# Attention followed by a SwiGLU block on one core: the attention output of batches 2 to 7 transposed by DMA through DRAM scratch, not by TensorE

## The chip, the cores and the metric

The kernel runs on one core of a Trainium2 chip. Its time is the device time of one execution in microseconds; the kernel before takes 408.24 us (median of 3 runs, 408.18 to 408.55). The core has a matrix engine (TensorE, PE in the profile), a vector engine (VectorE, DVE), an engine for activation functions (ScalarE, ACT), a general one (GpSimd, POOL), and a sync engine (SyncE, SP) that here only issues DMA transfers, in order. SBUF and PSUM are the on-chip memories; matmuls write to PSUM, which the kernel uses as 8 banks of 128 x 512 float32.

## What is computed

Causal attention with an extra bias from a running sum of `s`, in 8 batches of 8 heads, 576 positions of 64 elements; its output, with the heads of a position side by side, is the 4608 x 512 input of a gated feed-forward block (FFN). From the reference, shortened:

```python
# q, k, v: (8, 8, 576, 64), s: (8, 8, 576)
scores = scale * np.matmul(q, k.transpose(0, 1, 3, 2))
cum = np.cumsum(np.maximum(s, 0.0), axis=-1)
bias = -(cum[:, :, :, None] - cum[:, :, None, :])
scores = np.where(causal, -1000000000.0, scores + np.minimum(bias, 0.0))
attn = softmax(scores)                       # written out in the reference
attn_out = np.matmul(attn, v)
x = attn_out.transpose(0, 2, 1, 3).reshape(B * S, H * D)      # 4608 x 512
# w_gate, w_val: 512 x 1536; w_out: 1536 x 512
g = x @ w_gate
silu = g * (1.0 / (1.0 + np.exp(-g)))
out = (silu * (x @ w_val)) @ w_out           # 4608 x 512, float32
```

## The kernel before

The FFN works on 9 tiles of 512 tokens. Its first matmuls need `x` with the 512 features on the partitions, as `xt` (128 partitions x 4 pairs of heads x 512 tokens), while attention leaves the output of a pair of heads as `ot`, with the tokens on the partitions. So each pair's output has to be transposed. A batch has 576 tokens, so the pair's columns go to two tiles: batch `b` gives the last `512 - 64 b` tokens of tile `b` and the first `64 + 64 b` of tile `b + 1`.

Attention for one head is cut into pieces (4 of scores, 3 of the product with `v`), and a generator yields after each with its position in heads (`kk + 0.1` and so on). The FFN loop emits its own matmuls in 36 steps a tile and after each pumps the generator up to a target, so that the pieces of batch `tt + 1` stand between the matmuls of FFN tile `tt`. `LAG` is how many heads attention is to be ahead of the bare minimum when a tile starts. All engines run their instructions in the order of emission.

```python
def av_out(bh):                       # normalise one head: PSUM -> ot
    pr, e = divmod(bh, 2)
    if e == 0:
        ots[pr] = otp.tile([128, NCH, 2 * D], BF16, tag="ot", name="ot")
    ...
    nc.vector.reciprocal(rc, av3[:, :, D])                       # L401
    nc.vector.tensor_mul(ot[:, :, e * D : (e + 1) * D], ...)     # L402

def x_pe(pr):                         # transpose one pair: ot -> xt
    b, r = divmod(pr, H // 2)
    ot = ots.pop(pr)
    for tt in ((0, 1) if b == 0 else (b + 1,)):
        if r == 0:
            xts[tt] = xtp.tile([128, 4, TT], BF16, tag="xt", name="xt")
    bs = take()
    ps = view16(bs, S)
    for c in range(NCH):              # 5 chunks: 4 of 128 tokens, 1 of 64
        n = 128 if c < 4 else TAIL
        nc.tensor.transpose(                                     # L420
            ps[:, c * 128 : c * 128 + n], ot[0:n, c, :], ident[0:n, 0:n]
        )
    n0 = TT - 64 * b
    nc.vector.tensor_copy(xts[b + 1][:, r, 0 : S - n0], ps[:, n0:S])   # L424
    nc.vector.tensor_copy(xts[b][:, r, TT - n0 : TT], ps[:, 0:n0])     # L425
    give(bs)

def attn_items():
    for kk in range(H, BH + 2):
        h, step = divmod(kk, HB)
        if kk < BH:
            ...                       # scores of head kk; side(h, step): loads, casts,
                                      # scratch writes and DMA transposes of q and k
        x = kk - 2
        if x >= H and x % 2 == 1:
            x_pe(x // 2)
            yield kk + 0.5
        p = kk - 1
        if H <= p < BH:
            av_piece(p, (0, 1, 2))    # L385
            yield kk + 0.6
            av_piece(p, (3,))
            yield kk + 0.7
            av_piece(p, (4,))
            av_out(p)
            yield kk + 0.8

def ffn_items(tt):
    xt = xts[tt]
    for ft in range(NFT):             # 12 times
        for c in range(4):            # c: pair of heads
            nc.tensor.matmul(pg, WG[j][:, c, f0 : f0 + 128], xt[:, c, :], ...)  # L518
        ...                           # tanh on ScalarE, products on VectorE
        yield 1
        for c in range(4):
            nc.tensor.matmul(pv, WV[j][:, c, f0 : f0 + 128], xt[:, c, :], ...)  # L533
        ...
        yield 1
    for ts_ in range(4):              # 4 output blocks of 128 tokens
        for ft in range(NFT):
            nc.tensor.matmul(py, hts[ft][:, ts_ * 128 : (ts_ + 1) * 128], WO..., ...)  # L546
            ...
        nc.scalar.mul(ysb, py, 0.5)                              # L554
        nc.sync.dma_start(out[...], ysb)                         # L556
        yield 1

LAG = 1.65
for tt in range(NTT):
    lo = H * (tt + 1) + (LAG if tt else 0)
    hi = min(H * (tt + 2) + LAG, BH + 2)
    ...                               # pump from lo to hi over the 36 steps of tile tt
```

The scores are L347, their exponentials L360. From the sixth half batch on, q and k (as bfloat16) already go through DRAM scratch: GpSimd casts them, a DMA writes `ks` and `qs` (L244), and DMA transposes bring them back as `pk` and `pq` (L254). All of these are issued on the sync engine's queue.

Of the kernel before, what the change touches and what calls it, by code (L numbers as in the profile page):

```python
# [13 lines left out]
BF16 = mybir.dt.bfloat16  # L14
# [5 lines left out]
def kernel(  # L20
# [11 lines left out]
    nc = tc.nc  # L32
    PSUM = bass.MemoryType.PSUM

    B, H, S, D = q.shape
    NT, DM = out.shape
    DF = moe_w_gate.shape[1]
    BH = B * H
    NCH = 5
    TAIL = S - 512  # L40
# [5 lines left out]
    TT = 512  # L46
# [17 lines left out]
    def pt_col(tj, bi):  # L64
# [10 lines left out]
    xtp = ctx.enter_context(tc.tile_pool(name="xtp", bufs=3))  # L75
    hpool = ctx.enter_context(tc.tile_pool(name="hpool", bufs=3))
    yp = ctx.enter_context(tc.tile_pool(name="yp", bufs=3))
    dram = ctx.enter_context(
        tc.tile_pool(name="dram", bufs=1, space=bass.MemoryType.DRAM)
    )  # L80

    NPE = 5
    KS = {i: dram.tile([NR * S, 128], BF16, name=f"ks{i}") for i in range(NPE, NHB)}
    QS = {i: dram.tile([NR * S, 128], BF16, name=f"qs{i}") for i in range(NPE, NHB)}

    WG = [const.tile([128, 4, WCH], BF16, name=f"wg{j}") for j in range(NWCH)]
# [14 lines left out]
    with tc.manual_schedule():  # L101
# [14 lines left out]
        def take(kind="s"):  # L116
            b = min((x for x in bank if x[0] == kind), key=lambda x: released[x])
            assert released[b] < OPEN
            released[b] = OPEN
            return b  # L120

        def give(b):
            clock[0] += 1
            released[b] = clock[0]
# [15 lines left out]
        def view16(b, w):  # L140
            return bank[b][:, 0 : w // 2].bitcast(BF16)
# [12 lines left out]
        def load_qk(hb):  # L154
            load_one(hb, "k")
            load_one(hb, "q")
# [66 lines left out]
        def cast_one(hb, name, eng):  # L223
            cts[name, hb] = cp.tile([128, J, NR, D], BF16, tag="c" + name, bufs=2, name="c" + name)
            dst = cts[name, hb].rearrange("x j r d -> x r j d")
            src_t = loaded[name, hb]
            if eng is nc.scalar:
                nc.scalar.copy(dst, src_t)
            else:
                eng.tensor_copy(dst, src_t)  # L230
# [11 lines left out]
        def scratch(hb):  # L242
            for name, SC in (("k", KS), ("q", QS)):
                nc.sync.dma_start(  # L244
                    SC[hb].rearrange("(x j) c -> x (j c)", j=J),
                    cts[name, hb].rearrange("x j r d -> x (j r d)"),
                )
# [3 lines left out]
        def transposes(hb):  # L251
            for name, SC in (("k", KS), ("q", QS)):
                prs[name, hb] = cp.tile([128, NR * S], BF16, tag="p" + name, bufs=1, name="p" + name)
                nc.sync.dma_start_transpose(prs[name, hb], SC[hb])  # L254

        def split(hb, name, eng):
            kq = SRC[name][1]
            for r in range(NR):
                eng.tensor_copy(
                    KQ[hb % 2][r][64 * r : 64 * r + 64, kq, 0 : NR * S],  # L260
                    prs[name, hb][64 * r : 64 * r + 64, :],
                )
# [56 lines left out]
        ots = {}  # L319
        xts = {}  # L320
# [72 lines left out]
        def av_out(bh):  # L393
# [3 lines that stand above are left out]
            ot = ots[pr]  # L397
            av, bs = avs.pop(bh)
            av3 = av.rearrange("p (c e) -> p c e", e=D + 1)
            rc = small.tile([128, NCH], FP32, tag="rc", name="rc")  # L400
            nc.vector.reciprocal(rc, av3[:, :, D])  # L401
            nc.vector.tensor_mul(  # L402
                ot[:, :, e * D : (e + 1) * D],
                av3[:, :, 0:D],
                rc[:, :, None].to_broadcast([128, NCH, D]),
            )
            give(bs)
            pts.pop(bh)

        def x_pe(pr):  # L410
            b, r = divmod(pr, H // 2)
            ot = ots.pop(pr)
            for tt in ((0, 1) if b == 0 else (b + 1,)):
                if r == 0:
                    xts[tt] = xtp.tile([128, 4, TT], BF16, tag="xt", name="xt")
            bs = take()
            ps = view16(bs, S)
            for c in range(NCH):
# [9 lines that stand above are left out]
        def side(h, step):  # L428
# [8 lines left out]
            if h >= 3 and h + 3 < NHB and step == 0:  # L437
                load_qk(h + 3)
            if h + 1 < NHB and h + 1 >= NPE:
                if step == 0:  # L440
                    split(h + 1, "k", nc.vector)
                    aug(h + 1, SP4)
                if step == 1:
                    split(h + 1, "q", nc.vector)
            if h + 2 < NHB and h + 2 >= NPE:
                if step == 1:
# [32 lines left out]
# [4 lines that stand above are left out]
                    if step == 3 and h + 2 < NPE:  # L483
                        cast_one(h + 2, "k", nc.gpsimd)
                        cast_one(h + 2, "q", nc.gpsimd)
                    if step == 0 and 3 < h + 1 < NPE:
                        aug(h + 1, SP4)
                    for ci in range(4):
                        score_piece(kk, ci)
                        if ci == 1:  # L490
                            side(h, step)
                        yield kk + 0.1 + ci / 8
                        if h + 1 < NPE and (step, ci) in PREP_AT:
                            prep_one(h + 1, PREP_AT[step, ci])
                            yield kk + 0.1 + ci / 8
                x = kk - 2
                if x >= H and x % 2 == 1:
                    x_pe(x // 2)
                    yield kk + 0.5
                p = kk - 1  # L500
                if H <= p < BH:
                    av_piece(p, (0, 1, 2))
                    yield kk + 0.6
                    av_piece(p, (3,))
                    yield kk + 0.7
                    av_piece(p, (4,))
                    av_out(p)
                    yield kk + 0.8

        def ffn_items(tt):  # L510
# [111 lines left out]
        first_batch()  # L622
        second_psum()
        at = attn_items()
        state = {"pos": float(H)}

# [4 lines left out]
                except StopIteration:  # L631
                    state["pos"] = 1e9

        LAG = 1.65
        hook = {
            1: [lambda: cast_one(2, "k", nc.gpsimd), lambda: cast_one(2, "q", nc.vector)],
            2: [lambda: prep_one(2, 0)],
# [4 lines left out]
            21: [lambda: load_qk(5)],  # L642
        }
        for tt in range(NTT):
            lo = H * (tt + 1) + (LAG if tt else 0)
            hi = min(H * (tt + 2) + LAG, BH + 2)
            span = 36
            n0 = 7 if tt == 0 else 0
            n = 0
            for _ in ffn_items(tt):  # L650
                n += 1
                for f in hook.pop(n, ()):
                    f()
                pump(lo + (hi - lo) * min(1.0, max(0, n - n0) / (span - n0)))
# [31 lines left out]
```

The softmax here doesn't subtract the row's maximum and nothing guards it: scores larger than these inputs give would overflow.

## Time and profile before

| | |
|---|---|
| time, median of 3 | 408.24 us (408.18 to 408.55) |
| span of the profiled execution | 406.5 us |
| granted TensorE clock, mean | 0.987 |
| DMA moved | 56.71 MB, 140 GB/s in the mean |
| DMA packets | 85288, of which 65489 under 512 B |
| from one FFN tile's first matmul to the next, steady part | 42.1 us |

A group of the profile's fifth part is read like this: line, engine, operation, output from input, count, then busy time and mean length of one, then the idle time of the engine just before them and who ended it. For the operations that are changed:

```profile
L402 DVE TENSOR_TENSOR ot<-bank,rc 128x320 bf16<-128x320 f32 x56 | 27.5, 492 | 1.9
L424 DVE COPY xt<-bank 128x128 bf16<-128x128 bf16 (+6 forms) x28 | 9.0, 321 | 31.7 <-PE bank L420 31.0
```

The 31.7 us before L424 is VectorE's idle time, not TensorE's. Tiles are named after the buffers in the code; `bank` and `one` are PSUM banks.

### The profile page before, as it was taken

The page shows a single profiled execution, that of the slowest core. Times are in us where ns is not written, and L with a number is a line of the kernel's source. Part 1 is how long each engine was busy: PE and PEld are TensorE (multiplying, and loading weights), DVE is VectorE, ACT ScalarE, POOL GpSimd, SP SyncE. Part 2 cuts the span into 40 slices and gives each one's busy share as a digit, 9 for nine tenths or more (in the row PEclk, how much of TensorE's full clock was granted, in tenths as well). Part 3 has the DMA queues.
Part 4 walks back from the last instruction along what each step waited for, and adds up shares of the span by engine and source line. Part 5 has one row for each costly group of instructions (what it writes and reads, how often), then busy time and mean ns, then how long its engine had stood idle before and what let it go on. Part 6 is the DMA issues. An engine that isn't in the chain of part 4 may idle for free.

```text
span 406.5 us, 8052 instructions
## 1 busy us (share of the span) xinstructions
PE 384.8 (95%) x3100; PEld 213.0 (52%) x3100; DVE 249.1 (61%) x487; ACT 212.0 (52%) x407; POOL 125.0 (31%) x225
## 2 busy tenths in 40 slices
PE   2778799999999999999999999999999999999996
PEld 2664355655555555555555555555555554444442
DVE  7755658547863696368835784489447733852760
ACT  6742566855555655555545654655555542322321
POOL 6852444732442235222613162316211110000000
PEclk9988899999999999999999999999999999999999
DMA  7999899398635784579356944681510002002002
GB/s 242 188 250 212 267 192 269 133 272 190 178 93 194 174 206 118 173 194 211 102 157 192 247 72 127 214 167 51 120 57 0 2 27 78 0 16 89 2 1 103
DMA packets 85288, 56.71 MB, mean 140 GB/s; under 512 B 65489, under 2 KB 69553, under 8 KB 85249
## 3 DMA queue, kind: packets, MB, share of 16 engines
q1 hardware_dynamic: 81440, 51.44, 47.0%
q0 software_dynamic: 3808, 4.76, 6.9%
q8 instruction: 24, 0.39, 0.4%
q14 instruction: 16, 0.12, 0.1%
HBM read 37.90 MB, written 15.93 MB: 132 GB/s over the span
## 4 chain that ended last, share of the span: by engine, by line
PE 89%; DVE 4%; ACT 2%; DMA 2%; POOL 1%; issue 1%; ACTq 0%; SPq 0%
PE bank L546 23%; PE bank L518 22%; PE bank L533 22%; PE bank L347 9%; PE bank L385 7%; PE bank L420 3%; PE wide L347 1%; DMA kq<-HL 1%; PE one L385 1%; DMA s_sb<-in_s_dram 1%; ACT th L523 1%; POOL vt L171 1%; DVE pp L525 1%; DVE kq L301 1%; ACT pt L360 1%
## 5 line engine op out<-in xcount | busy, mean ns | idle before, releaser
L360 ACT ACTIVATE pt<-bank 128x512 bf16<-128x512 f32 x224 | 104.2, 505 | 42.4 <-PE bank L347 35.1
L525 DVE SCALAR_TENSOR_TENSOR pp<-th,bank 128x512 bf16<-128x512 bf16 x108 | 74.2, 687 | 65.2 <-ACT th L523 64.6
L518 PE MATMUL bank<-xt,wg 128*128 128x512 bf16 x432 | 112.1, 382 | 0.7 <-DVE xt L425 0.7
L533 PE MATMUL bank<-xt,wv 128*128 128x512 bf16 x432 | 112.5, 383 | 0.0
L523 ACT ACTIVATE th<-bank 128x512 bf16<-128x512 f32 x108 | 64.5, 597 | 81.6 <-PE bank L518 79.8
L546 PE MATMUL bank<-wo,ht 128*128 128x512 bf16 x432 | 105.7, 379 | 0.0
L363 POOL TENSOR_SCALAR_AFFINE_SELECT pt<-pt 128x512 bf16<-128x512 bf16 x64 | 40.8, 638 | 127.1 <-ACT pt L360 124.7
L538 DVE TENSOR_TENSOR ht<-pp,bank 128x512 bf16<-128x512 bf16 x108 | 73.8, 684 | 7.4
L347 PE MATMUL bank<-kq 128*128 128x128 bf16 (+4 forms) x504 | 66.7, 241 | 3.3 <-DVE kq L301 2.5
L347 PEld LDWEIGHTS <-kq 128*128 128x128 bf16 x576 | 46.1, 100 | 40.2 <-issue 4.2
L518 PEld LDWEIGHTS <-wg 128*128 128x128 bf16 x432 | 38.6, 98 | 36.9 <-issue 1.9
L533 PEld LDWEIGHTS <-wv 128*128 128x128 bf16 x432 | 38.9, 99 | 35.2 <-issue 1.7
L546 PEld LDWEIGHTS <-ht 128*128 128x128 bf16 x432 | 38.1, 98 | 34.9
L385 PEld LDWEIGHTS <-pt 128*128 128x128 bf16 x960 | 41.1, 98 | 19.0 <-issue 1.9
L385 PE MATMUL bank<-vt,pt 128*128 128x65 bf16 x840 | 44.0, 194 | 0.0
L554 ACT ACTIVATE ysb<-bank 128x512 f32<-128x512 f32 x36 | 21.5, 597 | 42.9 <-PE bank L546 41.4
L368 POOL TENSOR_SCALAR_AFFINE_SELECT pt<-pt 128x64 bf16<-128x64 bf16 x64 | 15.3, 239 | 63.4 <-ACT pt L360 60.7
L402 DVE TENSOR_TENSOR ot<-bank,rc 128x320 bf16<-128x320 f32 x56 | 27.5, 492 | 1.9
L424 DVE COPY xt<-bank 128x128 bf16<-128x128 bf16 (+6 forms) x28 | 9.0, 321 | 31.7 <-PE bank L420 31.0
L401 DVE RECIPROCAL rc<-bank 128x5 f32<-128x5 f32 x56 | 10.6, 190 | 25.2 <-PE bank L385 25.2
L171 POOL CAST vt<-rawv 128x512 bf16<-128x512 f32 (+1 forms) x40 | 25.8, 673 | 0.0
L230 POOL CAST ck<-rawk 128x1152 bf16<-128x1152 f32 x15 | 17.4, 1159 | 11.5 <-DMA rawk<-in_k_dram 11.5
(59 smaller groups left out, 191.6 us busy)
## 6 DMA issues: line engine op xcount, KB each, us to landing
out_dram<-ysb SPq DMA_DIRECT2D x36, 256.0 KB
rawk<-in_k_dram SPq DMA_DIRECT2D x15, 576.0 KB
rawq<-in_q_dram SPq DMA_DIRECT2D x15, 576.0 KB
rawv<-in_v_dram SPq DMA_DIRECT2D x32, 256.0 KB
ks<-ck SPq DMA_DIRECT2D x11, 288.0 KB
qs<-cq SPq DMA_DIRECT2D x11, 288.0 KB
wg<-in_moe_w_gate_dram POOLq DMA_DIRECT2D x2, 768.0 KB, 12.0
wv<-in_moe_w_val_dram POOLq DMA_DIRECT2D x2, 768.0 KB, 13.6
```

The lines of the kernel that those rows point to most:

```text
L171: eng.tensor_copy(VT[b % 2][0:n, c, :, 0:D], loaded["v", b][0:n, c, :, :])
L347: nc.tensor.matmul(sc[:, o : o + w], T[:, 1, e * S + 128 * tj : e * S + 128 * (tj + 1)], T[:, 0, e * S + lo : e * S + hi], start=True, sto ...
L360: nc.scalar.activation(pt[:, c0 : c0 + W], sc[:, 0:W], AF.Exp, scale=0.125)
L363: nc.gpsimd.affine_select(pt[:, 1088:1600], pt[:, 1088:1600], pattern=[[0, 4], [1, 128]], compare_op=ALU.is_ge, fill=zreg, base=0, channel ...
L385: nc.tensor.matmul(av[:, bi * (D + 1) : (bi + 1) * (D + 1)], pt[:, c0 : c0 + 128], VT[b % 2][:, tj, h, :], start=(tj == 0), stop=(tj == bi),)
L402: nc.vector.tensor_mul(ot[:, :, e * D : (e + 1) * D], av3[:, :, 0:D], rc[:, :, None].to_broadcast([128, NCH, D]),)
L518: nc.tensor.matmul(pg, WG[j][:, c, f0 : f0 + 128], xt[:, c, :], start=(c == 0), stop=(c == 3),)
L523: nc.scalar.activation(th, pg, AF.Tanh, scale=0.5)
L525: nc.vector.scalar_tensor_tensor(pp, in0=th, scalar=1.0, in1=pg, op0=ALU.add, op1=ALU.mult)
L533: nc.tensor.matmul(pv, WV[j][:, c, f0 : f0 + 128], xt[:, c, :], start=(c == 0), stop=(c == 3),)
L538: nc.vector.tensor_mul(ht, pp, pv)
L546: nc.tensor.matmul(py, hts[ft][:, ts_ * 128 : (ts_ + 1) * 128], WO[ft // WKO][:, ft % WKO, :], start=(ft == 0), stop=(ft == NFT - 1),)
```

## The change

From batch 2 on (`XB = 2`), a pair's output isn't transposed by TensorE. `x_out` writes `ot` to a DRAM scratch `XS` of 576 x 128 with two DMAs, once both heads are normalised. `x_in` later reads it back with two DMA transposes, straight into the two `xt` tiles. That takes the transposes from TensorE, the copies from VectorE and the bank from PSUM, and puts four DMAs on the sync queue in their place. Batches 0 and 1 are transposed as before. The constant lag becomes a list that rises to 2.5 heads, to leave time for the way through DRAM before a tile of the FFN starts. The first batch's own code is the same in both kernels.

```diff
     NPE = 5
+    XB = 2
     KS = {...}
+    XS = {
+        i: dram.tile([S, 128], BF16, name=f"xs{i}") for i in range(XB * H // 2, BH // 2)
+    }
...
+        def x_out(pr):
+            ot = ots.pop(pr)
+            nc.sync.dma_start(
+                XS[pr][0:512].rearrange("(c p) d -> p c d", p=128), ot[:, 0:4, :]
+            )
+            nc.sync.dma_start(XS[pr][512:S], ot[0:TAIL, 4, :])
+
+        def x_tiles(b, r):
+            for tt in ((0, 1) if b == 0 else (b + 1,)):
+                if r == 0:
+                    xts[tt] = xtp.tile([128, 4, TT], BF16, tag="xt", name="xt")
+
+        def x_in(pr):
+            b, r = divmod(pr, H // 2)
+            n0 = TT - 64 * b
+            x_tiles(b, r)
+            nc.sync.dma_start_transpose(xts[b][:, r, TT - n0 : TT], XS[pr][0:n0])
+            nc.sync.dma_start_transpose(xts[b + 1][:, r, 0 : S - n0], XS[pr][n0:S])
+
         def x_pe(pr):
...
-                if x >= H and x % 2 == 1:
+                if H <= x < XB * H and x % 2 == 1:
                     x_pe(x // 2)
                     yield kk + 0.5
+                if XB * H <= x < BH and x % 2 == 1:
+                    x_in(x // 2)
                 p = kk - 1
...
                     av_piece(p, (4,))
                     av_out(p)
+                    if p >= XB * H and p % 2 == 1:
+                        x_out(p // 2)
                     yield kk + 0.8
...
-        LAG = 1.65
+        LAGS = [0, 1.65, 1.65, 1.9, 2.2, 2.5, 2.5, 2.5, 2.5, 2.5]
...
-            lo = H * (tt + 1) + (LAG if tt else 0)
-            hi = min(H * (tt + 2) + LAG, BH + 2)
+            lo = H * (tt + 1) + LAGS[tt]
+            hi = min(H * (tt + 2) + LAGS[tt + 1], BH + 2)
```

More of the change, by code (lines that the diff above doesn't have):

```diff
@@ L412, in x_pe @@
             ot = ots.pop(pr)
-            for tt in ((0, 1) if b == 0 else (b + 1,)):
-                if r == 0:
-                    xts[tt] = xtp.tile([128, 4, TT], BF16, tag="xt", name="xt")
+            x_tiles(b, r)
             bs = take()
```

## The prediction

> **What bounds the kernel now.** I read the page's busy shares first, then a table of busy time by stretches of 40 us, then the chain that ended last, and last the timeline around one transposition. Part 1 of the page:
>
> ```profile
> PE 384.8 (95%) x3100; PEld 213.0 (52%) x3100; DVE 249.1 (61%) x487; ACT 212.0 (52%) x407; POOL 125.0 (31%) x225
> ```
>
> TensorE is busy 95% of the span, VectorE 61%, ScalarE 52%. The average hides that the stages differ, so here is the table by stretches (columns: length, then busy us and instruction count of PE, PEld, DVE, ACT, POOL; granted clock; DMA share; GB/s):
>
> ```profile
> 0.00:50.00 50.00, 33.52 (x340) 23.09 (x341) 31.60 (x60) 28.37 (x40) 28.19 (x55) 0.91 0.97 235
> ...
> 90.00:130.00 40.00, 40.00 (x336) 22.26 (x335) 26.78 (x54) 22.10 (x45) 13.78 (x24) 1.00 0.63 170
> 130.00:170.00 40.00, 40.00 (x346) 22.40 (x344) 26.87 (x56) 21.99 (x46) 13.32 (x24) 1.00 0.58 153
> ...
> 250.00:290.00 40.00, 40.00 (x341) 22.33 (x340) 25.79 (x53) 22.91 (x47) 13.92 (x25) 1.00 0.57 141
> ```
>
> TensorE's gaps lie in the first 50 us, which the change doesn't touch. From 90 to 330 us it never stops: every stretch reads 40.00 of 40.00, at full clock. There an instruction taken from TensorE shortens the run by its whole length, and a wait put before TensorE lengthens it by the whole wait. The chain says the same, and gives the transposes' share (L420 is the transpose of `x_pe`):
>
> ```profile
> PE 89%; DVE 4%; ACT 2%; DMA 2%; POOL 1%; issue 1%; ACTq 0%; SPq 0%
> PE bank L546 23%; PE bank L518 22%; PE bank L533 22%; PE bank L347 9%; PE bank L385 7%; PE bank L420 3%; PE wide L347 1%; DMA kq<-HL 1%; PE one L385 1%; DMA s_sb<-in_s_dram 1%; ACT th L523 1%; POOL vt L171 1%; DVE pp L525 1%; DVE kq L301 1%; ACT pt L360 1%
> ```
>
> L420 on banks is 28 pairs of heads. 3% of 406.5 us is 12.2 us (10.2 to 14.2 with the rounding), 0.36 to 0.51 us a pair. The timeline gives it exactly (start, busy, operation):
>
> ```profile
> 119.32 1.03 PE L546 MATMUL bank<-wo,ht 128*128 128x512 bf16 x4
> 120.18 0.52 PE L420 MATMUL bank<-ident,ot 128*128 128x128 bf16 x5
> 120.64 0.48 PE L385 MATMUL bank<-vt,pt 128*128 128x65 bf16 x10
> 120.95 1.03 PE L546 MATMUL bank<-wo,ht 128*128 128x512 bf16 x4
> ```
>
> The busy times overlap, since matmuls are pipelined, so cost is read from start to start: five transposes of one pair hold TensorE from 120.18 to 120.64, 0.46 us. Six other pairs that I read gave 0.45 or 0.46. Likewise four 512-wide matmuls cost 0.86 us (119.32 to 120.18) and ten of L385 0.31.
>
> **What the Trainium skill says.** (1) "TensorE: Matmul & The Clock Gate", Part 4: PE-mode transpose: the output goes to PSUM and needs a copy out afterwards, and a 128x128 transpose took about 275 ns in one kernel. The trace agrees on the copies (L424, L425); one transpose lasts 219 ns, but a stream of five costs 0.46 us, so its figure would overstate the saving threefold. (2) "DMA: Bandwidth & Descriptors", Two DMAs through the same engine are not ordered: a DMA that reads what another wrote must have its issuing engine wait for the first one's completion. The trace shows it on the existing scratch path of q and k (below). (3) Same page, Anatomy of one DMA: about 2 us fixed cost, mostly completion; stated for the other issuing path, but the trace has 2.16 us for such a write here. (4) Same page, Specifications: under 512 B a transfer loses line rate. The new writes have runs of 256 B; no separate number for that in this trace.
>
> **The change part by part.** *Removed:* 24 pairs (4 in each of batches 2 to 7) times 5 transposes on TensorE. All lie in the stretch where TensorE never pauses: 24 x 0.455 = **10.9 us less**. Also 48 VectorE copies of some 0.2 to 0.4 us each, about 15 us, and 24 uses of a PSUM bank. VectorE is at two thirds there (26.8 of 40) and TensorE waited for `xt` once, 0.7 us, so I count these as nothing.
>
> *Added:* 48 scratch writes and 48 DMA transposes of 24 x 147 KB each way, on the sync queue. Bytes are cheap: the DMA share falls from 0.6 to 0.08 over these stretches. What counts is latency before a tile of the FFN, and the order on the sync queue, for which the existing q/k path is the model (SPq lines are issues):
>
> ```profile
> 156.55 0.36 SPq L244 DMA_DIRECT2D qs<-cq  x1
> 157.01 1.28 SPq L254 DMA_TRANSPOSE pk<-ks  x1
> 159.07 1.23 SPq L254 DMA_TRANSPOSE pq<-qs  x1
> 163.10 4.06 SPq L556 DMA_DIRECT2D out_dram<-ysb  x2
> ```
>
> The `qs` write was issued until 156.91, and the transpose that reads it could start at 159.07: 2.16 us for write and completion. A table of DMA share in half microseconds shows the second transpose's traffic ending at about 161.5, 2.5 us after its issue began: some 1.4 us until data flows and 1.1 us for 1152 rows. The new ones have 64 to 384 rows where the waiting tile is concerned: 1.4 + up to 0.4 + about 0.2 for the completion, an estimate of 2.0 us.
>
> *Moved:* the pump's lag rises from 1.65 to 1.9, 2.2 and 2.5 heads, so that attention runs up to 0.85 heads (a tile lasts 42.1 us, 131.47 to 173.57 between two tiles' first matmuls, so a head 5.3) further ahead of the FFN: room for the round trip. It moves work between tiles, and TensorE is full in all of them: no gain or loss by itself.
>
> Now each FFN start, from the built order of instructions. In TensorE's stream only the fourth matmul of the tile needs the batch's last pair, so three (0.65 us) still run. The trap is that the sync queue works in order and the tile's output stores (`out<-ysb`) stand ahead of the transposes.
> - *Tile 2* (lag still 1.65): the stores of the 3rd and 4th output block of tile 1 both stand before the transpose of pair 11. So it waits for the last matmul of tile 1, ScalarE's scaling (0.75 us with hand-over), the store's issue (0.4), then 2.0 for itself: 3.2 us. TensorE has ten L385 (0.31) and three matmuls (0.65) to do: 0.96. **Stall 2.2 us.**
> - *Tile 3*: only the 3rd block's store stands ahead. TensorE still has 0.22 + 0.86 + 0.25 + 0.86 + 0.31 + 0.86 + 0.15 + 0.23 + 0.65 = 4.4 us against 3.2: no stall. *Tile 4*: 4.2 against 3.2, none. *Tiles 5 and 6*: a whole output block more, none.
> - *Tile 7*: attention ends just before. From the last L385 of head 63: VectorE 0.9, two write issues 0.7, landing 2.1, transpose 1.9 = 5.6 us; TensorE has 24 + 3 matmuls at 0.215 = 5.8. Even: 0.4 as an allowance. *Tile 8*: none.
>
> Sum: 408.2 - 10.9 + 2.2 + 0.4, and 0.6 for traffic in the way of one or two of these trips = **400.5 us**, 1.9% less.
>
> **The rivals.** *A: the round trips hide nearly everywhere and the whole 10.9 us arrive*, at 397 us, perhaps 396 where fewer copies and banks in use also help. For it: TensorE-bound stretches without one gap, lags raised step by step for this purpose. Against: tile 2's lag is unchanged and its transposes stand behind the last store. *B: the wait before the FFN takes the place of the transposes.* For it: loads of 1.15 MB of q and k are issued at each half batch on the same 16 DMA engines (at 200 to 380 GB/s, 3 to 6 us), and of the five transposes that the trace shows waiting for their write, four could start 2.0 to 2.4 us after the write's issue, but one, at 245.42, only 4.3 us after it. If tiles 2, 3, 4 and 7 each lost 2 us more than worked out, the time would be about 408, no gain at all. Against: the last loads before a tile start are issued some 7 us ahead. *C: the sync queue becomes the bound*, since it now blocks twice per pair for a write to complete, and q/k preparation, `aug` rows and stores come later. Its issues now fill some 10 us of the 21 us of a half batch (four heads); four writes and four transposes more add 3 to 4, and their waits as much, so it stays below its limit, and q and k are prepared four heads ahead. It would make 405 to 412 and show as TensorE waiting for `kq`. I give it little.
>
> **Range and chances.** The saving is firm: 10.9, give or take 0.5. The stalls are the doubt: 0 at best, 3 as worked out, 8 or more under rival B. So 8 times in 10 between 396.8 and 404.5, the middle at 400.5. The line of 2% faster is at 400.1, nearly in the middle: 0.45 faster by over 2%, 0.51 within 2%, 0.04 slower by over 2%.
>
> **What would show it.** Right: no TensorE transposes of `ot` after batch 1 and PE's instructions down by 120; L424/425-type copies down to 16; one TensorE wait of 1.5 to 3 us for a DMA of `xt` at the start of tile 2 (near 130 us), under 1 us at the others; stretches between tiles full as before. Wrong: waits for `xt` at most tile starts (B); waits for `kq` (C); or no wait at tile 2 (A). If TensorE's other work slowed, by a clock below 1.00 or by longer start-to-start times, the sum would be wrong in a way that I don't expect.

## The result, and the profile after

The changed kernel took 413.58 us (median; 413.12 to 414.87), the kernel before, beside it, 408.21 us (407.33 to 408.55). The ratio is 1.014, with a 95% interval of 1.011 to 1.017: slower by 1.4%. The prediction said 400.5 us, between 396.8 and 404.5.

The profile's first and fourth part, after:

```profile
PE 379.7 (92%) x2980; PEld 208.1 (50%) x2980; DVE 237.1 (58%) x439; ACT 212.6 (52%) x407; POOL 125.6 (30%) x225
...
PE 84%; DMA 5%; DVE 4%; ACT 3%; issue 2%; POOL 1%; SPq 0%; ACTq 0%; DVEq 0%; POOLq 0%
PE bank L571 22%; PE bank L558 21%; PE bank L543 21%; PE bank L351 9%; PE bank L389 6%; DMA xs<-ot 2%; DMA xt<-xs 2%; PE wide L351 1%; ACT th L548 1%; DVE kq L305 1%; DVE pp L550 1%; ACT pt L364 1%; DMA rawq<-in_q_dram 1%; ACT kq L303 1%; PE one L389 1%
```

TensorE has 120 instructions fewer, and the transposes of `ot` (3% of the chain before) are gone from the chain. In their place stand the two halves of the way through DRAM, `xs<-ot` and `xt<-xs`, 2% each. The table by stretches (columns as in the prediction) shows where:

```profile
130.00:170.00 40.00, 34.95 (x275) 19.00 (x275) 23.44 (x44) 19.84 (x40) 11.92 (x21) 0.91 0.64 164
170.00:210.00 40.00, 36.43 (x287) 19.52 (x286) 22.25 (x43) 20.21 (x43) 13.41 (x23) 0.91 0.68 177
210.00:250.00 40.00, 37.91 (x307) 20.84 (x306) 21.94 (x43) 21.67 (x45) 14.11 (x23) 0.96 0.80 197
250.00:290.00 40.00, 40.00 (x345) 22.24 (x343) 25.11 (x48) 23.36 (x48) 15.04 (x26) 1.00 0.73 177
```

Before, the stretches from 90 to 330 us read 40.00 at clock 1.00. Now three of them have gaps, and in the same three the granted clock is below 1. From 250 us on all is as predicted. The list of TensorE's waits (us in total, times, longest) names the gaps:

```profile
PE bank L543 <- DMA xt<-xs: 11.1, 3, 5.4
```

These are the starts of tiles 2, 3 and 4, at 5.44, 3.57 and 2.09 us. The timeline of TensorE at the first of them (start, busy, operation, idle time before and who ended it):

```profile
128.79 0.81 PE L543 MATMUL bank<-xt,wg 128*128 128x512 bf16 x3
135.05 0.59 PE L543 MATMUL bank<-xt,wg 128*128 128x512 bf16 x1 [5.44 <-DMA xt<-xs]
...
136.13 1.91 PE L558 MATMUL bank<-xt,wv 128*128 128x512 bf16 x4
137.83 0.63 PE L351 MATMUL bank<-kq 128*128 128x448 bf16 x2
```

Three matmuls of the tile run, the fourth needs the batch's last pair and waits. Then four 512-wide matmuls hold TensorE from 136.13 to 137.83, 1.70 us, where four cost 0.86 us before: half speed. Here are the stretches of low clock. At the first two it falls while TensorE still waits, at the third 1.1 us after the wait (the clock is the column behind the counts):

```profile
132.70:139.00 6.30, 3.95 (x18) 1.92 (x18) 1.97 (x4) 1.69 (x3) 1.73 (x2) 0.50 0.32 106
180.60:187.00 6.40, 5.60 (x22) 2.45 (x22) 1.41 (x3) 2.40 (x5) 0.24 (x1) 0.50 0.81 214
227.00:231.00 4.00, 4.00 (x29) 2.18 (x28) 1.37 (x2) 1.36 (x4) 0.24 (x1) 0.62 0.84 252
```

So each of these three waits is paid twice, as a gap and then as a slow stretch. **The balance of the two profiled spans** (406.5 and 412.3 us, +5.8):

| | us |
|---|---|
| transposes gone (the prediction's 24 x 0.455) | -10.9 |
| TensorE idle: 406.5 - 384.8 = 21.7 before, 412.3 - 379.7 = 32.6 after | +10.9 |
| TensorE's busy time above what the saving leaves: 379.7 - (384.8 - 10.9) | +5.8 |

The waits for `xt` (11.1) are the whole of the second row. The third is about the half clock: 3.95 and 5.60 us at 0.50 and 4.00 at 0.62 lose 2.0 + 2.8 + 1.5 = 6.3.

Why was `xt` late? The timeline of the sync queue at the same place (SPq lines are issues):

```profile
125.11 0.43 SPq L151 DMA_DIRECT2D rawk<-in_k_dram  x1
125.59 0.50 SPq L151 DMA_DIRECT2D rawq<-in_q_dram  x1
126.19 2.94 SPq L189 DMA_DIRECT2D kq<-HL  x4
129.23 0.39 SPq L416 DMA_DIRECT2D xs<-ot  x1
129.67 0.53 SPq L419 DMA_DIRECT2D xs<-ot  x1
130.30 1.78 SPq L581 DMA_DIRECT2D out_dram<-ysb  x2
132.67 1.16 SPq L430 DMA_TRANSPOSE xt<-xs  x1
```

VectorE had finished the pair's `ot` at 125.35. Its write was issued at 129.23, 3.9 us later, behind the next half batch's loads of q and k (two issues) and four `aug` transfers (`kq<-HL`, rows that carry the bias into the operands of the scores; 2.94 us of issue). At tiles 3 and 4 it was 3.5 and 3.8 us. From the write's issue to its landing the chain counts 3.4 us here, then 2.3 for the transpose. In the kernel before, the loads were issued at 125.12 and the tile's first matmul came at 131.47, 6.4 us later; now it comes at 128.79, 3.7 us later.

The other new cost is on the queue itself. The durations of the transposes' issues (count, then ns at least, median, at most):

```profile
L430 SPq DMA_TRANSPOSE xt<-xs x24: 1116/1160/2082, 102.3 to 344.3; - x24
L431 SPq DMA_TRANSPOSE xt<-xs x24: 1172/1196/2436, 104.1 to 345.5; - x24
```

The two writes took 0.39 and 0.57 us in the median of 24 each. That is 0.39 + 0.57 + 1.16 + 1.20 = 3.3 us of issue for a pair, 6.6 for a half batch of 21 us. Between 100 and 290 us the sync queue's waits add up to 122.7 us in the kernel before and to 38.6 after: of 190 us it was occupied for 67, and is now for 151 (190 less the waits).

### The profile page after: what moved, and what is told of

Its sections match the earlier page's. It is cut to its first block, busy times and chain, and to the rows that moved or that the text cites. A ratio compares the mean times of both kernels' runs of the same rounds, so it can differ in the third digit from the quotient of the medians.

```text
span 412.3 us, 7923 instructions
## 1 busy us (share of the span) xinstructions
PE 379.7 (92%) x2980; PEld 208.1 (50%) x2980; DVE 237.1 (58%) x439; ACT 212.6 (52%) x407; POOL 125.6 (30%) x225
## 4 chain that ended last, share of the span: by engine, by line
PE 84%; DMA 5%; DVE 4%; ACT 3%; issue 2%; POOL 1%; SPq 0%; ACTq 0%; DVEq 0%; POOLq 0%
PE bank L571 22%; PE bank L558 21%; PE bank L543 21%; PE bank L351 9%; PE bank L389 6%; DMA xs<-ot 2%; DMA xt<-xs 2%; PE wide L351 1%; ACT th L548 1%; DVE kq L305 1%; DVE pp L550 1%; ACT pt L364 1%; DMA rawq<-in_q_dram 1%; ACT kq L303 1%; PE one L389 1%
## 5 line engine op out<-in xcount | busy, mean ns | idle before, releaser
L364 ACT ACTIVATE pt<-bank 128x512 bf16<-128x512 f32 x224 | 105.5, 504 | 50.1 <-PE bank L351 34.7
L543 PE MATMUL bank<-xt,wg 128*128 128x512 bf16 x432 | 114.3, 386 | 11.8 <-DMA xt<-xs 11.1
L558 PE MATMUL bank<-xt,wv 128*128 128x512 bf16 x432 | 114.0, 387 | 0.0
L351 PE MATMUL bank<-kq 128*128 128x128 bf16 (+4 forms) x504 | 68.6, 244 | 3.6 <-DVE kq L305 2.9
L389 PEld LDWEIGHTS <-pt 128*128 128x128 bf16 x960 | 44.5, 100 | 30.1 <-issue 8.6
L571 PEld LDWEIGHTS <-ht 128*128 128x128 bf16 x432 | 38.5, 98 | 35.7
L234 POOL CAST ck<-rawk 128x1152 bf16<-128x1152 f32 x15 | 17.8, 1188 | 11.8 <-DMA rawk<-in_k_dram 11.8
L303 ACT COPY kq<-bank 64x640 bf16<-64x640 bf16 (+1 forms) x12 | 8.8, 736 | 14.3 <-DVE kq L305 14.3
```

The costliest lines, as they stand in the source:

```text
L351: nc.tensor.matmul(sc[:, o : o + w], T[:, 1, e * S + 128 * tj : e * S + 128 * (tj + 1)], T[:, 0, e * S + lo : e * S + hi], start=True, sto ...
L364: nc.scalar.activation(pt[:, c0 : c0 + W], sc[:, 0:W], AF.Exp, scale=0.125)
L389: nc.tensor.matmul(av[:, bi * (D + 1) : (bi + 1) * (D + 1)], pt[:, c0 : c0 + 128], VT[b % 2][:, tj, h, :], start=(tj == 0), stop=(tj == bi),)
```

## The experiments

Two theories. **Lateness**: the pair's write stands behind loads and `aug` on the queue that works in order, so the round trip ends late at the tile starts; earlier writes or more lag would recover the 10.9 us. **The queue**: the sync queue is nearly full, and stops at a transpose until the write that it reads has landed (14 of the 24 times, 13.1 us); more lag or another order only moves the wait, to q and k, which go through the same queue. A third claim is common to both: the clock's loss follows from the standstill.

Each short diff is against the changed kernel. Ratios are to the kernel before, run beside it, with 95% intervals. The start-up varies: over the profiled executions TensorE's first matmul of tile 0 comes between 33.9 and 38.5 us (34.4 both before and after the change). Where a profile is to be compared to 1 or 2 us, I therefore count from that matmul to the end of TensorE's last: 368.4 us before, 374.2 after.

### Where it happens, and the clock

**from_batch5**: DMA transposes only from batch 5 on.

```diff
-    XB = 2
+    XB = 5
```

> Only batches 5 to 7 go through DRAM, the lags stay as in the changed kernel. Theory (the loss is the waits for xt at tiles 2, 3 and 4 and the clock that falls after them; the way through DRAM itself is free): 12 pairs x 0.455 = 5.5 us saved, no wait for xt by DMA, clock as before: 402.7 us (402 to 403.5). Rival (the added DMA work slows the whole run, or the raised lags cost something): no gain or a loss, 407 to 410 us.

Measured: 406.0 us, 0.994 (0.992 to 0.996). A gain, but of 2.2 us against the 408.2 that the expectation started from (2.6 against the runs beside it), and not 5.5. One wait for `xt` appeared, 1.6 us at tile 5, now the first such tile. Counted from tile 0, the profile has 364.4 us: 4.0 less than before, which is the 5.5 saved less the wait (368.4 - 5.5 + 1.6 = 364.5). The clock stayed at 1.00 after this wait. Why the medians gain less isn't shown; in the profiled execution the start-up was 3.8 us longer than in that of the kernel before.

**lags_only**: all pairs transposed by TensorE, the new lags kept.

```diff
-    XB = 2
+    XB = 8
```

> All pairs transposed by TensorE as before; only the list of lags of the changed kernel. Theory (the lags by themselves cost nothing; the loss lies in the way through DRAM): as before, ratio 0.998 to 1.003. Rival (running attention further ahead disturbs the other engines): ratio 1.005 or more, with new waits of TensorE in tiles 2 to 5.

Measured: 409.23 us, 1.0015 (0.9986 to 1.0043), no wait for `xt`. The lags by themselves cost nothing that can be seen.

**filled**: 24, 16 and 9 matmuls of 512 columns without use are put before the fourth matmul of tiles 2, 3 and 4, so that TensorE doesn't stand still there.

```diff
+                    if ft == 0 and c == 3 and tt in FILL:  # {2: 24, 3: 16, 4: 9}
...
+                        for _ in range(FILL[tt]):
+                            nc.tensor.matmul(<idle bank>, ...)
```

> The changed kernel, with idle work for TensorE in front of the fourth matmul of tiles 2, 3 and 4: 24, 16 and 9 matmuls of 512 columns into a bank that nobody reads (5.2, 3.4 and 1.9 us). The waits of 5.4, 3.6 and 2.1 us are then filled, not shortened. Theory (the clock falls because TensorE stood still): the clock stays at 1.00 through all three tile starts and some 5.7 us come back, 408 us (406.5 to 409.5). Rival (the clock falls for another reason, such as the DMA traffic or the load of the stage): the clock still falls, and the time stays at 413 us or above.

Measured: 414.15 us, 1.015 (1.008 to 1.022). The stretch of tile 2:

```profile
130.00:170.00 40.00, 40.00 (x318) 21.57 (x316) 22.84 (x43) 21.47 (x44) 13.49 (x24) 1.00 0.69 186
```

The clock reads 1.00 in all three stretches, where it was 0.91, 0.91 and 0.96. So the clock had fallen because TensorE stood still. The sum agrees: waits for `xt` of 4.2 us were left (0.7 at tile 3, 1.2 at tile 4, 2.4 at tile 5), the filling is 49 x 0.215 = 10.5, and 368.4 - 10.9 + 10.5 + 4.2 = 372.2; the profile counted from tile 0 has 372.5, with nothing left for a lower clock. After the change the same sum needs the 5.8 (368.4 - 10.9 + 11.1 + 5.8 = 374.4, against 374.2). A gain in the median didn't show, and only 1.7 us were to be had: filling and waits together are 14.7 us in place of 11.1.

After the wait of 2.4 us at tile 5 the clock did not fall:

```profile
270.74 0.39 PE L551 MATMUL bank<-xt,wg 128*128 128x512 bf16 x1 [2.38 <-DMA xt<-xs]
```

Not every wait of this length is paid twice, then. In all profiles together, from 90 us on, TensorE stood still 54 times for 1 us or more. Half clock came during the wait or after it in all 24 cases of 3.37 us or more, in none of the 17 up to 1.95, and in 9 of the 13 between 2.09 and 3.33.

### The order on the sync queue

**aug_later**: from half batch 6 on, the four `aug` issues come after the pair's transposes.

```diff
-                    aug(h + 1, SP4)
+                    if h < 5:
+                        aug(h + 1, SP4)
...
+                if step == 1 and 5 <= h and h + 1 < NHB:
+                    aug(h + 1, SP4)
```

> The changed kernel with its own lags; from half batch 5 on, the four small aug transfers (2.9 us of issue on the sync queue) are issued after the transposes of the pair, not ahead of its writes. Theory (the last pair's writes came late because they stood behind these issues): the writes go out some 3 us earlier; tile 2 then waits only for the output store that stands ahead of its transposes, some 2.5 us in place of 5.4; tiles 3 and 4 wait 0 to 0.5 us; with a shorter spell of low clock 402 us (400.5 to 404). Rival (the writes wait for their data, or the trips are slow by traffic, not by their place in the queue): waits and time nearly as in the changed kernel, 411 to 414 us.

Measured: 432.25 us, 1.060 (1.054 to 1.065); waits for `xt` of 24.8 us. The sync queue at tile 2:

```profile
129.70 0.50 SPq L151 DMA_DIRECT2D rawq<-in_q_dram  x1
130.30 0.41 SPq L416 DMA_DIRECT2D xs<-ot  x1
130.76 0.55 SPq L419 DMA_DIRECT2D xs<-ot  x1
131.41 1.04 SPq L584 DMA_DIRECT2D out_dram<-ysb  x2
136.76 1.14 SPq L430 DMA_TRANSPOSE xt<-xs  x1
```

The write now stands directly behind the 1.15 MB of loads, and the transpose can start only 5.4 us after its issue ended (131.31 to 136.76). The queue stands still meanwhile and holds back q and k: VectorE's waits for `pk` rose from 6.2 to 22.5 us. Against the expectation, the slow `aug` issues had been useful as distance between the loads and the write: behind them, in the changed kernel, the same step took 2.5 us (130.20 to 132.67).

**loads_later**: the loads instead of the `aug` rows come after the transposes.

```diff
-            if h >= 3 and h + 3 < NHB and step == 0:
+            if 3 <= h < 5 and step == 0:
...
+                if step == 1 and 5 <= h and h + 3 < NHB:
+                    load_qk(h + 3)
```

> The changed kernel with its own lags; from half batch 5 on the loads of q and k (1.15 MB, a burst of 5 to 6 us on the DMA engines) are issued after the transposes of the pair at step 1, not ahead of its writes at step 0. Theory after the first runs (the pair's writes land only when the burst of loads in front of them on the same queue is done): the last pair's writes land 2.2 to 2.5 us after their issue instead of 3.4 to 5.4, the waits at tiles 2, 3 and 4 sum to 6 to 8 us instead of 11.1, the clock falls less: ratio 0.995 to 1.008. Rival (the sync queue is full of issues, whatever their order): the burst and the issues only move, q/k preparation comes later and VectorE waits for pk; ratio 1.010 or more.

Measured: 430.85 us, 1.050 (1.042 to 1.058); 21.8 us of waits for `xt`, 28.1 for `pk`. The write did land sooner, as the expectation said: 2.2 us at tile 2 (issued at 132.14, the transpose at 134.31). But it was issued 2.0 us after the tile's first matmul (130.14), behind `aug`, and the burst now stands in front of the scratch writes of q and k.

**write_first**: loads and `aug` both come directly after the pair's writes, ahead of its transposes.

```diff
                         x_out(p // 2)
+                    if step == 0 and h >= 5:
+                        if h + 3 < NHB:
+                            load_qk(h + 3)
+                        if h + 1 < NHB:
+                            aug(h + 1, SP4)
```

(and both taken out of their old place)

> The changed kernel with its own lags and its own place of the transposes; only the loads of q and k and the four aug transfers are issued after the pair's writes and not ahead of them. The write at tile 2 goes out some 3.9 us earlier and lands while the queue issues the loads; the transposes still stand behind 4 us of issues and behind the burst of loads. Order alone is the cause: waits at tiles 2, 3 and 4 under 4 us in all, ratio 0.980 to 0.992. Order needs the larger lag too (the trip is 7 us or more with all that the queue issues in it): waits of 6 to 9 us in all, ratio 0.998 to 1.008.

Measured: 415.16 us, 1.017 (1.013 to 1.020); waits for `xt` of 10.4 us. The write is early, but the transposes stand behind the loads and `aug`. This order doesn't cure lateness at these lags.

**loads_pool**: the loads of q, k and v go through GpSimd's queue.

```diff
-    nc.sync.dma_start(<rawk, rawq, v>)
+    (nc.gpsimd if hb >= 6 else nc.sync).dma_start(<rawk, rawq>)
+    (nc.gpsimd if b >= 2 else nc.sync).dma_start(<v>)
```

> The changed kernel with its own lags; the loads of q and k from half batch 6 on and of v from batch 2 on are issued from GpSimd's queue, so that they neither take issue time on the sync queue (some 4 us of each 21 us) nor stand in front of the writes on it. Both theories of what is late (burst in front, full queue) expect fewer waits: at tile 2 some 3 us, at tiles 3 and 4 under 1 us, ratio 0.980 to 0.992. If it is the DMA engines' total traffic that stretches the trips, the waits stay: ratio 1.010 or more.

Measured: 425.42 us, 1.030 (1.021 to 1.040). Here, in loads_pool_lag28 and in read_late the median takes in executions over 1.5% slower than the fastest (two of four, two of four, three of twenty), and the ratio leaves them out. **loads_pool_lag28** has the lag of the next section as well:

> As loads_pool, with the lag at 2.8 heads from tile 2 on. Theory: with the queue relieved, the larger lag covers the whole trip; no wait for xt, no wait of VectorE for pk, clock 1.00: ratio 0.973 to 0.980 (10.9 us saved, up to 2 us of small waits). Rival (total traffic): waits as in lag28, ratio near 1.00.

Measured: 430.02 us, 1.037 (1.025 to 1.049). No wait for `xt` is left, but 25.2 us of VectorE's waits for `pk` and 21.2 us of TensorE's for VectorE. GpSimd, which also casts q, k and v, was busy for 163.8 us in place of 125.6. That its casts came late is the likely reason; it wasn't tested apart.

### More lag: does the wait go, or move?

**lag28**: 2.8 heads at all tiles from 2 on.

```diff
-        LAGS = [0, 1.65, 1.65, 1.9, 2.2, 2.5, 2.5, 2.5, 2.5, 2.5]
+        LAGS = [0, 1.65] + [2.8] * 8
```

> The changed kernel with the lag at 2.8 heads from tile 2 on, in place of 1.65, 1.9, 2.2 and 2.5. Theory (the trips are only late against the tile start): tile 2 starts 1.15 heads, some 6 us, later against attention, tile 3 some 4.7 us, tile 4 some 3 us, each more than its wait: no wait is left, the clock stays up, 408.2 - 10.9 = 397.3 us (396.5 to 399). Rival (the trips stretch with the traffic, so that they are late whatever the lag): waits of some us stay at some tiles, over 401 us.

Measured: 409.47 us, 1.003 (1.000 to 1.005), 12 us above what lateness expected. TensorE's waits, and then VectorE's:

```profile
PE bank L543 <- DVE pp L550: 5.4, 4, 1.7
PE bank L543 <- DMA xt<-xs: 4.9, 4, 2.7
```

```profile
DVE kq L263 <- DMA pk<-ks: 21.3, 9, 5.1
```

The waits for `xt` fell from 11.1 to 4.9, but VectorE now waits 21.3 us (6.2 after the change, 0.5 before it) for the transposed k, and TensorE then 5.4 us for VectorE, whose product for the FFN (`pp`) stands behind the copy of `pk` (copy at 149.00, `pp` at 149.95, TensorE's wait over at 150.69). The wait moved. The clock stayed at 1.00, and the two lines, 10.3 us, eat up the saving of 10.9. The profiled execution, 412.91 us, is among the slowest of the 20.

Why `pk` is late can be read from its transposes. Before the change they were issued 7.7 to 9.3 us ahead of VectorE's copy, between 90 and 290 us; in lag28 3.7 to 5.0 us ahead, with the waits in it. The issue comes too late on the queue; how far traffic also stretches the way isn't separated.

**shadow_lag28**: TensorE transposes all pairs as before the change, and the writes and DMA transposes are issued as well, into tiles that nobody reads.

```diff
-                if H <= x < XB * H and x % 2 == 1:
+                if H <= x and x % 2 == 1:
                     x_pe(x // 2)
...
-            nc.sync.dma_start_transpose(xts[b][:, r, TT - n0 : TT], XS[pr][0:n0])
+            nc.sync.dma_start_transpose(sh0[:, TT - n0 : TT], XS[pr][0:n0])
```

> TensorE transposes every pair, as before; the 48 writes and 48 DMA transposes of the changed kernel are issued as well, on the sync queue in the same places, into a tile that nobody reads; lag 2.8 from tile 2 on. Nothing waits for the trips. Theory S (the sync queue is nearly full: from 100 to 290 us it was idle 122.7 us before and 38.6 us in the changed kernel; what is issued late, above all q and k for the coming heads, then stops VectorE and through it TensorE): slower than before, ratio 1.008 to 1.025, VectorE waits some 20 us for pk as in lag28. Rival L (only the latency of the trips ahead of a tile start costs time): ratio 0.998 to 1.004.

Measured: 414.46 us, 1.013 (1.009 to 1.018). Of VectorE's waits in this run:

```profile
DVE kq L264 <- DMA pk<-ks: 17.3, 8, 3.8
```

TensorE waits 4.2 us for VectorE (`pp`). TensorE waits for no round trip here, and still the 96 DMAs cost 1.3%, by way of q and k. That is the queue theory without the latency; it holds both the issues and the queue's stops for the writes (12.0 us between 100 and 290 us). A lag of 2.8 without any of the DMAs wasn't run; lags_only went up to 2.5.

### The queue's stops

**other_scratch_lag28**: as lag28, but the transposes read a scratch that was written long before, so that they needn't wait for the pair's write. All DMAs remain; the output holds other data than the reference's.

```diff
-            nc.sync.dma_start_transpose(xts[b][:, r, TT - n0 : TT], XS[pr][0:n0])
+            nc.sync.dma_start_transpose(xts[b][:, r, TT - n0 : TT], KS[NPE][0:n0])
```

(the second transpose likewise)

> As lag28, but the DMA transposes into xt read a scratch of k that was written long before, not the pair's own; the writes are still issued. So xt holds other data (the output is not the reference's), with the same number and size of transfers. The sync queue no longer stops to wait for a write (9.4 us of its 100 to 290 us in lag28). Theory S in its strict form (the issues themselves fill the queue): only a part comes back, ratio 0.990 to 1.000, VectorE still waits over 10 us for pk. If the stops for the writes are what counts: ratio 0.973 to 0.983.

Measured: 402.68 us, 0.983 (0.977 to 0.989), with these waits of TensorE and of VectorE:

```profile
PE bank L543 <- DVE pp L550: 2.5, 4, 1.3
...
PE bank L543 <- DMA xt<-ks: 1.2, 1, 1.2
```

```profile
DVE kq L263 <- DMA pk<-ks: 16.2, 9, 4.1
```

Against lag28 the ratio falls by 0.020: at this lag the stops for the pair's write are worth 2%. TensorE's busy time is 374.0, just what 384.8 - 10.9 leaves. The strict form of the queue theory was right about `pk`, 16.2 us of waits, and wrong about the time. The queue was occupied for 168 of its 190 us from 100 to 290 us, more than in lag28 (155), and yet the kernel was faster. So neither a queue as full as this nor 16 us of VectorE's waits for `pk` costs much by itself; what counts is the part that reaches TensorE, 3.7 us here against 10.3.

**other_scratch**: the same with the change's own lags.

> The changed kernel with its own lags; the transposes into xt read a scratch of k written long before, so that the queue doesn't stop for the pair's own write (the output is not the reference's). If the stop is the cause: TensorE waits only at tile 2, some 2 us for the store ahead of the transposes, as first worked out, and the clock falls little or not: ratio 0.975 to 0.987. If the issues by themselves are the cause: waits at three tiles, ratio over 1.000.

Measured: 409.89 us, 1.004 (1.002 to 1.006); three waits for `xt`, 8.5 us. Here the stops are worth only 1%: the transposes still come late, behind loads and `aug` (131.95 at tile 2, against 132.67).

Three attempts moved the transposes away from their write. **read_late** reads one head later, with a lag of 3.3:

```diff
-                if XB * H <= x < BH and x % 2 == 1:
-                    x_in(x // 2)
+                xl = kk - 3
+                if XB * H <= xl < BH and xl % 2 == 1:
+                    x_in(xl // 2)
```

> The transposes into xt are issued one head later (three heads after the pair's second, not two), so that the write has landed when the queue reaches them, and the lag is 3.3 from tile 2 on. All data right. Theory S: the stops go, the issues stay: ratio 0.988 to 1.000, as other_scratch_lag28. Rival L: waits gone, ratio 0.973 to 0.980.

Measured: 408.22 us, 0.997 (0.994 to 1.000); `xt` 7.8 us, `pk` only 1.4. The queue now stopped ahead of them, at scratch writes of q and k that wait for GpSimd's casts. **acts** adds the writes one step later, and writes and stores from ScalarE's queue:

```diff
-            nc.sync.dma_start(
+            nc.scalar.dma_start(
                 XS[pr][0:512].rearrange("(c p) d -> p c d", p=128), ot[:, 0:4, :]
```

> As read_late, and the pair's two writes (one step later, when ot is long ready) and all output stores are issued from ScalarE's queue: some 23 + 16 us of issue leave the sync queue, and its stops for ysb. Same traffic. Theory S: the queue has room again; no wait for xt, VectorE waits under 8 us for pk, TensorE without gaps: ratio 0.973 to 0.985. Rival T (the DMA engines' traffic stretches everything, whoever issues it): no better than read_late, ratio 0.995 or more.

Measured: 423.43 us, 1.034 (1.026 to 1.042). The sync queue is relieved, but stops for 38 us (of 100 to 290 us) at scratch writes that wait for GpSimd, with the transposes behind them: 17.8 us of waits for `xt`. **read_before** takes the writes and stores back to the sync queue, as in the changed kernel, and issues the transposes at the start of that step, ahead of those scratch writes, with a lag of 3.0:

```diff
                 h, step = divmod(kk, HB)
+                xl = kk - 3
+                if XB * H <= xl < BH and xl % 2 == 1:
+                    x_in(xl // 2)
```

> Data right. The transposes of a pair are issued half a head later than in the changed kernel and still ahead of the q/k scratch writes; lag 3.0. Between the pair's writes and its transposes the queue has only a store, so where the queue is late it still stops for the write: ratio 0.990 to 1.000. If only the distance in attention's time counts (1.3 heads, 6.8 us): 0.973 to 0.982.

Measured: 406.38 us, 0.995 (0.993 to 0.997); `xt` 2.2 us, `pk` 17.9. With all DMAs and the right data it is 0.5% faster than before.

### A version that keeps more of the gain

**rearranged**: read_before, with the loads and `aug` issued between a pair's writes and its transposes, as in write_first.

> Data right. As read_before, with the loads of q and k and the four aug transfers moved between the pair's writes and its transposes: the write goes ahead of the burst of loads, and the queue issues for some 4 us while it lands. Stop theory: few stops for xs (under 3 us in all from 100 to 290 us), few waits of TensorE, ratio 0.973 to 0.985. Against it: the transposes now follow the burst of loads and may land late; then waits for xt at tiles 2 to 5 and ratio 0.99 or more.

Measured: 403.86 us, 0.989 (0.982 to 0.996). Between 100 and 290 us no stop for `xs` is left, against 8.1 us in read_before, as the stop theory said. The interval still overlaps that of read_before. **rearranged_stores_act**: also the output's stores from ScalarE's queue.

```diff
-                nc.sync.dma_start(
+                nc.scalar.dma_start(
                     out[tt * TT + ts_ * 128 : tt * TT + (ts_ + 1) * 128, :], ysb
```

> As rearranged, with the output stores issued from ScalarE's queue: 16 us of issue and the stops for ysb leave the sync queue. If the queue's fill still matters: 0.003 to 0.008 better than rearranged. If only the stops for the write matter: the same within 0.003.

Measured: 399.75 us, 0.981 (0.975 to 0.987), the lowest median of all. The intervals of the two overlap, so what the stores add isn't settled. The profiled execution, at 404.46 us, is the slowest of the four; the others took 399.4 to 399.8. Its sync queue, where it now does other work between write and read:

```profile
125.47 0.58 SPq L416 DMA_DIRECT2D xs<-ot  x1
126.10 0.53 SPq L419 DMA_DIRECT2D xs<-ot  x1
126.67 0.59 SPq L151 DMA_DIRECT2D rawk<-in_k_dram  x1
...
127.90 2.92 SPq L189 DMA_DIRECT2D kq<-HL  x4
132.92 1.15 SPq L430 DMA_TRANSPOSE xt<-xs  x1
```

The write goes out ahead of the loads, and in most half batches the transpose follows the last `aug` issue at once. At tile 2, shown here, the queue still stops for 2.1 us ahead of the transpose (130.82 to 132.92; the profile puts it down to the landing of `rawk`), and the transpose itself lands after 4.2 us, against 2.3 in the changed kernel. So one wait for `xt` is left, 3.4 us at tile 2, and 7.9 us of VectorE's waits for `pk`. **rearranged_acts_lag33** raises the lag to 3.3:

> rearranged_stores_act with the lag at 3.3 heads in place of 3.0, 1.6 us more for the last trip. If its wait of 3.4 us at tile 2 is a matter of distance: half of it goes, ratio 0.974 to 0.981. If the queue's own delay moves with it: the same as with 3.0, 0.978 to 0.984.

Measured: 404.7 us, 0.992 (0.989 to 0.994). The wait for `xt` is gone, but TensorE waits 5.3 us for VectorE (`pp`). More lag doesn't help further.

## Why the prediction was wrong

**Right:** the saving. TensorE's busy time falls by 10.9 us as worked out from start-to-start times (374.0 in other_scratch_lag28), where no half clock hides it. Right too: the lags are free (lags_only), tiles 5 to 8 have no stall, and the sync queue's order decides tile 2.

**Wrong, the stalls' sum.** It had 2.2 at tile 2, none at tiles 3 and 4, 0.4 at tile 7. Measured: 5.44, 3.57, 2.09 and none. The failed step is what stands on the sync queue ahead of the transposes: "So it waits for the last matmul of tile 1, ScalarE's scaling (0.75 us with hand-over), the store's issue (0.4), then 2.0 for itself: 3.2 us", and the same 3.2 at tiles 3 and 4. I followed only the output stores and took the pair's write for landed. The loads, the `aug` issues and the write stood there too: the write was itself 3.5 to 3.9 us late on the same queue, and took another 2.5 to 3.4 to land. At tile 2 the landing was the smaller part: where nothing had to wait for it (other_scratch), the transposes were issued only 0.7 us earlier. The argument that put rival B away, that the loads are issued "some 7 us ahead", was roughly right for the kernel before (6.4 at tiles 2 to 4) and wrong for the changed one: at tile 2 it was 3.7 us, and in front of the write.

**Wrong, the queue's load.** Rival C was put away with "four writes and four transposes more add 3 to 4" us per half batch. They add 6.6, since a transpose's issue hardly shrinks with its rows: medians of 1.16 and 1.20 us for 64 to 512 rows, against 1.32 for the 1152 rows of `pk`. By the queue's waits, its occupied part of a half batch went from 7.4 us, not "some 10", to 16.7 of 21. The Trainium skill, "DMA: Bandwidth & Descriptors", section Issuing engines are not separate DMA queues, calls the time to initiate a DMA usually small relative to the DMA; here the trace differs, 1.16 us of issue in the 2.3 us of a transpose, and the issues are what fills the queue. C's mechanism appeared as soon as lag hid the stalls (lag28, shadow_lag28), more by the stops for the writes, which the prediction also named, than by the issues (other_scratch_lag28). Its sign differed from the one named: VectorE waiting for `pk`, and TensorE then for VectorE.

**Missing: the clock.** 5.8 us come from TensorE at half clock after the stalls. The Trainium skill, "TensorE: Matmul & The Clock Gate", section Why this matters for your kernels, warns of gaps in TensorE's work above about 3 us. The waits of 5.44 and 3.57 us agree; here a wait of 2.09 us was followed by it too (clock 0.62 from 227 to 231 us), as were 8 of the 12 others between 2.09 and 3.33 us. A predicted stall of 2.2 us should have had such a term, as a chance.

In numbers: 400.5 + (11.1 - 2.2 - 0.4) + 5.8 - 0.6 for the allowance for traffic = 414.2, against 413.58.

**Open:** how much of the loss at the change's own lags is the queue's fill and how much the stops, beyond the 1% of other_scratch; how much of `pk`'s waits, up to 5.1 us in lag28, is its late issue and how much traffic; and why half clock follows some waits of 2 to 3.3 us and not others.

## What to carry to other kernels

Moving work from a full engine to DMAs also loads the queue that issues them: add up its issues for a period and look at who stands ahead of each, the write as well as the read. Put a dependent write in front of bulk loads, and other issues between it and the DMA that reads it; here this helped only together with more lag (0.989 and 0.981, against 1.017 for write_first). Expect a stall of TensorE of more than some 2 us to cost more than itself, since the clock may drop with it; here it always did from 3.37 us on (in the changed kernel 11.1 us of waits cost 16.9).

## What the runs showed of the hardware

- The issue of a DMA transpose cost 1.16 and 1.20 us (medians of 24) for 64 to 512 rows, and 1.32 for 1152 (median of 11): almost fixed.
- A small write issued directly behind 1.15 MB of loads could be read only 5.4 us after the end of its issue (aug_later), against 2.16 us on the path that the prediction showed.
- TensorE's clock fell to half at waits of 5.44, 3.57 and 2.09 us, and came back 3.4 to 6.8 us after it fell. Matmuls without use, put in the place of the wait, kept it at 1.00. It did not fall after waits of 2.38 (filled), 2.65 (lag28), 2.70 (loads_pool) and 3.33 us (other_scratch), nor after any of 1.95 us or less.
